# A rebuilt prologue, four units in flight and a first MLP block in halves, in a fused recurrent-attention and MLP kernel

## The chip, the cores and the metric

The kernel runs on one core of one Trainium2 chip. The metric is the time of one execution on the device, in microseconds (us), as a median over several executions. The profile takes one execution; its span is about 1.7 us shorter than the time of that same execution (226.5 against 228.2 before the change), so spans are compared with spans and times with times. "Granted clock" is the share of its full clock that TensorE was given, as the trace records it. All executions quoted here are in the fast state of the chip, but for one, which is named.

## The reference

A linear recurrence (RWKV-5) over 768 steps for 4 sequences of 8 heads with 48 channels, then an MLP with SiLU on all 3072 tokens. Cut to what matters:

```python
for t in range(S):
    kt, vt, rt = (k[:, :, t].copy(), v[:, :, t].copy(), r[:, :, t].copy())
    cur = np.einsum('bhd,bhe->bhde', u[None] * kt, vt)
    y[:, :, t] = np.einsum('bhd,bhde->bhe', rt, state + cur)
    state = w[None, :, :, None] * state + np.einsum('bhd,bhe->bhde', kt, vt)
# y, as x of 3072 x 384, goes into the MLP:
h = x @ w_in                      # 384 x 2048
g = h * (1.0 / (1.0 + np.exp(-h)))
out = g @ w_out                   # 2048 x 384
```

## The kernel before

The steps are cut into chunks of 128. A **unit** is one chunk of one sequence: 24 units, and the four units of a chunk together make one MLP **block** of 512 tokens. Each unit goes through these parts:

- "natural" products on GpSimd: ku = k·u, rku_f = r·ku, kc = k times decay powers, and, after a sum on VectorE, vu = v·rku;
- p1: r and k are transposed on TensorE (tr, tk) and scaled by decay powers on VectorE (rT, kT);
- p2: the masked attention matrix (ae, ao);
- p3: the output y and the new state st (sps is the matmul part, sdec the decayed old state, stb its half-precision copy);
- p4: y is transposed (yT) and copied by ScalarE into the MLP's input xT.

The block's matmuls (hps with w_in, ops with w_out) are "fillers": pieces that the unit loop drops between the parts of later units. In all the timelines TensorE runs everything in the order in which it is written here.

The setup, with four buffers per input, and the decay powers from logarithms and exponentials on ScalarE:

```python
    rin = [big.tile([128, H, 64], FP, name=f"rin{i}") for i in range(NIN)]
    kin = [big.tile([128, H, 64], FP, name=f"kin{i}") for i in range(NIN)]
    vin = [big.tile([128, H, D], FP, name=f"vin{i}") for i in range(NIN)]
    kc = [big.tile([128, H, 64], F16, name=f"kc{i}") for i in range(2)]
    for i in range(NIN):
        nc.vector.memset(rin[i][:, :, D:64], 0.0)
        nc.vector.memset(kin[i][:, :, D:64], 0.0)
    for i in range(2):
        nc.vector.memset(kc[i][:, :, D:64], 0.0)
    # ... cut ...
    def load(i):
        if i >= NU:
            return
        sc, b = unit(i)
        for t, src, wd in ((rin, r, 64), (kin, k, 64), (vin, v, D)):
            nc.sync.dma_start(out=t[i % NIN][:, :, 0:D],
                              in_=src[b, :, sc * C:sc * C + C, :]
                              .rearrange("h t d -> t h d"))

    load(0)
    nc.sync.dma_start(out=w_bc, in_=bass.AP(tensor=w.tensor, offset=0,
                                            ap=[[0, 128], [1, HD]]))
    nc.sync.dma_start(out=u_bc, in_=bass.AP(tensor=u.tensor, offset=0,
                                            ap=[[0, 128], [D, H], [1, D]]))
    for i in range(1, NIN):
        load(i)
    # ... cut ...
    lamR = cst.tile([PR, NP, C], FP)
    nc.scalar.activation(out=lamR, in_=eR, func=AF.Exp)
    lamK = cst.tile([PR, NP, C], FP)
    nc.scalar.activation(out=lamK, in_=eK, func=AF.Exp, scale=-1.0)
    lamC = cst.tile([128, H, D], FP)
    nc.scalar.activation(out=lamC.rearrange("p h d -> p (h d)"), in_=lnw_bc,
                         func=AF.Exp, scale=it_rev)
    wCT = cst.tile([PR, NP], FP)
    nc.scalar.activation(out=wCT, in_=lnwT, func=AF.Exp, scale=float(C))
```

The natural products and the start of the transposes:

```python
    def p1_natural(i):

        n = i % NIN
        L = live.setdefault(i, {})
        L["v16"] = wrk.tile([128, H, D], F16, name="v16", bufs=3)
        nc.scalar.copy(out=L["v16"], in_=vin[n])
        ku = wrk.tile([128, H, D], FP, name="ku")
        nc.gpsimd.tensor_tensor(out=ku, in0=kin[n][:, :, 0:D], in1=u_bc, op=ALU.mult)
        rku_f = wrk.tile([128, H, D], FP, name="rku_f")
        nc.gpsimd.tensor_tensor(out=rku_f, in0=rin[n][:, :, 0:D], in1=ku, op=ALU.mult)
        nc.gpsimd.tensor_tensor(out=kc[i % 2][:, :, 0:D], in0=kin[n][:, :, 0:D],
                                in1=lamC, op=ALU.mult)
        rku = wrk.tile([128, H], FP, name="rku")
        nc.vector.tensor_reduce(out=rku, in_=rku_f, axis=mybir.AxisListType.X, op=ALU.add)
        L["vu"] = wrk.tile([128, H, D], FP, name="vu")
        nc.gpsimd.tensor_tensor(out=L["vu"], in0=vin[n],
                                in1=rku.unsqueeze(2).broadcast_to([128, H, D]),
                                op=ALU.mult)

    def p1(i):
        n = i % NIN
        L = live.setdefault(i, {})
        tr = ps.tile([128, NP, C], FP, tag="tA", bufs=3)
        tk = ps.tile([128, NP, C], FP, tag="tA", bufs=3)
        for t, src in ((tr, rin), (tk, kin)):
            flat = src[n].rearrange("p h d -> p (h d)")
    # ... cut ...
        L["rT"] = wrk.tile([PR, NP, C], FP, name="rT")
        nc.vector.tensor_tensor(out=L["rT"], in0=tr[0:PR], in1=lamR, op=ALU.mult)
        L["kT"] = wrk.tile([PR, NP, C], FP, name="kT")
        nc.vector.tensor_tensor(out=L["kT"], in0=tk[0:PR], in1=lamK, op=ALU.mult)
        if i >= B:
            L["rT16"] = wrk.tile([PR, NP, C], F16, name="rT16")
            nc.scalar.copy(out=L["rT16"], in_=L["rT"])
```

The state, the copy into the MLP's input, and the first MLP layer:

```python
        L["y16"] = wrk.tile([128, H, D], F16, name="y16")
        nc.vector.tensor_tensor(out=L["y16"], in0=y, in1=L["vu"], op=ALU.add)
        if sc < NCH - 1:
            if sc:
                sdec = wrk.tile([PR, NP, PW], FP, name="sdec")
                nc.gpsimd.tensor_tensor(out=sdec, in0=st[b],
                                        in1=wCT.unsqueeze(2).broadcast_to([PR, NP, PW]),
                                        op=ALU.mult)
            for p0, c0 in ((0, 0), (64, D)):
                dst = st[b][p0:p0 + D, :, c0:c0 + D]
                if sc:
                    nc.vector.tensor_tensor(out=dst, in0=sps[p0:p0 + D, :, c0:c0 + D],
                                            in1=sdec[p0:p0 + D, :, c0:c0 + D], op=ALU.add)
                else:
                    nc.vector.tensor_copy(out=dst, in_=sps[p0:p0 + D, :, c0:c0 + D])
            nc.gpsimd.tensor_copy(out=st16[b], in_=st[b])
    # ... cut ...
        yT = ps.tile([128, NQ, C], F16, tag="y", bufs=2)
        yf = L["y16"].rearrange("p h d -> p (h d)")
        for q in range(NQ):
            nc.tensor.transpose(yT[:, q, :], yf[:, 128 * q:128 * q + 128], ident16)
        nc.scalar.copy(out=xts[sc][:, :, b, :], in_=yT)
    # ... cut ...
    def l1(sc, ft):
        if ft == 0:
            gts[sc] = wrk.tile([128, NFT, B * C], F16, name="gT", bufs=2)
        hps = ps.tile([128, B * C], FP, tag="moe", bufs=3)
        for q in range(NQ):
            nc.tensor.matmul(hps, win[q][:, ft * 128:(ft + 1) * 128],
                             xts[sc][:, q, :, :].rearrange("p b t -> p (b t)"),
                             start=(q == 0), stop=(q == NQ - 1))
        nc.scalar.activation(out=gts[sc][:, ft, :], in_=hps, func=AF.Silu)
```

The order of everything. The w_in weights go out (three DMAs with a cast, issued by GpSimd) right after the first unit's products, the w_out weights (four DMAs) in the second unit; a block's pieces become available only when all its four units are done:

```python
    def moe(sc):
        for ft in range(NFT):
            yield lambda ft=ft: l1(sc, ft)
        for b in range(B):
            for part in range(4):
                yield lambda b=b, part=part: l2(sc, b, part)

    fillers = []

    def fill(n):
        for _ in range(n):
            if fillers:
                fillers.pop(0)()


    p1_natural(0)
    for q in range(NQ):
        nc.gpsimd.dma_start(out=win[q], in_=moe_w_in[128 * q:128 * q + 128, :])
    p1(0)
    for i in range(NU):
        p2(i)
        fill(2)
        if i == 1:
            for g in range(4):
                nc.gpsimd.dma_start(
                    out=wout[:, 4 * g:4 * g + 4, :],
                    in_=moe_w_out[512 * g:512 * g + 512, :]
                    .rearrange("(f p) n -> p f n", p=128))
        if i + 1 < NU:
            p1_natural(i + 1)
            p1(i + 1)
        load(i + NIN)
        fill(1)
        p3(i)
        fill(2)
        p4(i)
        fill(3)
        sc, b = unit(i)
        if b == B - 1:
            fill(len(fillers))
            fillers.extend(moe(sc))
    fill(len(fillers))
```

## Time and profile before

| | before |
|---|---|
| time, median of 3 (lowest to highest) | 228.23 us (226.78 to 228.32) |
| span of the profiled execution | 226.5 us |
| first MLP matmul (hps) starts | 42.84 us |
| from there to the end | 183.7 us |
| mean granted TensorE clock | 0.955 of full speed |

The prediction below shows the page's slices and the main lines of the timelines. One view is added: the list of TensorE's waits in the kernel before. The columns are the matmul group that waited, what released it, and then the total in us, how many waits, and the longest.

```profile
PE yT L237 <- DVE y L211: 9.4, 4, 4.5
PE ae L179 <- DVE kT L169: 6.1, 1, 6.1
PE tr L165 <- DMA rin<-in_r_dram: 5.1, 1, 5.1
```

All of these waits lie before 42.84 us. A summary by stretch says the same of the rest. Its columns are the stretch, its length, then the busy time (and the number of instructions) of TensorE, its weight loads, VectorE, ScalarE and GpSimd, then the granted clock, the DMA share and GB/s:

```profile
0.00:42.84 42.84, 22.29 (x180) 18.49 (x180) 22.38 (x52) 10.57 (x19) 27.81 (x43) 0.79 1.01 184
42.84:226.50 183.66, 179.97 (x1494) 114.57 (x1492) 93.46 (x173) 83.59 (x155) 91.15 (x108) 0.99 0.35 81
```

In the second stretch TensorE is busy for 179.97 of 183.66 us, and the 3.7 us that it is not are the tail after the last matmul. A change that leaves TensorE's work as it is, like this one, can save time only in the first stretch, where TensorE idles for 20.6 us.

### The profile page before, as it was taken

Reading aid. Unit: us, or ns where it says so; the run is one execution under the profiler, and the core shown is the slowest. Engines: PE = TensorE matmul, PEld = TensorE weight load, DVE = VectorE, ACT = ScalarE, POOL = GpSimd, SP = SyncE. Lnnn points to the kernel's source line nnn. Section 1 sums busy time; section 2 is a strip of 40 time slices with the busy share of each in tenths; the row PEclk is TensorE's granted clock in tenths of the full one; section 3 lists DMA queues with packets and bytes.
Section 4 is the critical chain, followed back from the end, with each engine's and each line's share of the span. In section 5 each row is a group of like instructions: output and inputs, shape, how many; then the busy total and the mean of one; then the engine's idle time right before and its main releaser. Section 6 shows DMA issues by size and latency. Waiting matters only on the chain.

```text
span 226.5 us, 4378 instructions
## 1 busy us (share of the span) xinstructions
PE 202.3 (89%) x1672; PEld 133.1 (59%) x1672; DVE 115.8 (51%) x225; ACT 94.2 (42%) x173; POOL 119.0 (53%) x150
## 2 busy tenths in 40 slices
PE   1266298799999999999999999999999999999993
PEld 1164177456667656766665776666676557654561
DVE  6157365647368536656833865563685256420020
ACT  2521011586621378411578211866213783029500
POOL 2387975765674665667467466656746561000000
PEclk9999555799999999999999999999999999999999
DMA  5999999992216385026735053923161000110011
GB/s 95 201 196 208 204 185 176 224 186 50 58 38 139 105 177 104 3 76 137 166 77 107 0 142 98 213 48 61 38 142 69 3 0 3 69 53 16 3 69 69
DMA packets 81604, 22.69 MB, mean 100 GB/s; under 512 B 75824, under 2 KB 81200, under 8 KB 81584
## 3 DMA queue, kind: packets, MB, share of 16 engines
q1 hardware_dynamic: 79040, 19.28, 39.3%
q0 software_dynamic: 2544, 3.15, 8.0%
q8 instruction: 13, 0.21, 0.4%
q14 instruction: 7, 0.06, 0.1%
HBM read 20.84 MB, written 4.72 MB: 113 GB/s over the span
## 4 chain that ended last, share of the span: by engine, by line
PE 81%; POOL 8%; DVE 3%; issue 3%; DMA 2%; SPq 1%; DVEq 0%; POOLq 0%
PE hps L248 28%; PE ops L260 28%; PE ae L179 10%; PE tr L165 4%; PE tk L165 4%; PE yT L237 2%; DMA u_bc<-in_u_dram 2%; POOL ku L145 2%; PE y L201 2%; POOL rku_f L147 2%; PE sps L208 2%; PE y L198 2%; POOL wout L292 1%; SPq L102 1%; POOL kc L148 1%
## 5 line engine op out<-in xcount | busy, mean ns | idle before, releaser
L248 PE MATMUL hps<-xT,win 128*128 128x512 f16 x288 | 70.2, 384 | 0.0
L251 ACT ACTIVATE gT<-hps 128x512 f16<-128x512 f32 x96 | 57.4, 598 | 29.5 <-PE hps L248 27.3
L260 PE MATMUL ops<-wout,gT 128*128 128x384 f16 x384 | 69.0, 326 | 0.0
L260 PEld LDWEIGHTS <-gT 128*128 128x128 f16 x384 | 35.8, 98 | 21.2
L248 PEld LDWEIGHTS <-win 128*128 128x128 f16 x288 | 26.7, 99 | 26.5 <-issue 1.3
L186 DVE TENSOR_TENSOR am<-ae,maskM 128x512 f16<-128x512 f32 x24 | 16.6, 691 | 49.1 <-PE ao L181 49.1
L153 POOL TENSOR_TENSOR vu<-vin,rku 128x384 f32<-128x384 f32 x24 | 19.9, 829 | 35.8 <-DVE rku L151 35.8
L179 PE MATMUL ae<-rT,kT 48*128 48x128 f32 x192 | 30.8, 306 | 6.1 <-DVE kT L169 6.1
L179 PEld LDWEIGHTS ae<-rT,kT 48*128 48x128 f32 x192 | 25.8, 206 | 14.2 <-issue 7.5
L264 DVE COPY osb<-ops 128x384 f32<-128x384 f32 x24 | 13.4, 557 | 38.3 <-PE ops L260 37.9
L181 PE MATMUL ao<-rT,kT 48*128 48x128 f32 x192 | 30.8, 306 | 0.0
L238 ACT COPY xT<-yT 128x384 f16<-128x384 f16 x24 | 11.4, 476 | 43.3 <-PE yT L237 43.3
L145 POOL TENSOR_TENSOR ku<-kin,u_bc 128x384 f32<-128x384 f32 x24 | 24.1, 1005 | 7.9 <-DMA u_bc<-in_u_dram 6.7
L172 ACT CAST rT<-rT 112x512 f16<-112x512 f32 x20 | 12.4, 618 | 37.2 <-DVE rT L167 37.2
L181 PEld LDWEIGHTS ao<-rT,kT 48*128 48x128 f32 x192 | 25.8, 206 | 0.0
L147 POOL TENSOR_TENSOR rku_f<-rin,ku 128x384 f32<-128x384 f32 x24 | 24.0, 999 | 1.9
L148 POOL TENSOR_TENSOR kc<-kin,lamC 128x384 f16<-128x384 f32 x24 | 24.0, 999 | 0.8 <-ACT lamC L130 0.8
L225 POOL CAST stb<-st 112x384 f16<-112x384 f32 x20 | 10.1, 503 | 25.0 <-DVE st L221 19.9
L165 PE MATMUL tr<-ident,rin 128*112 128x128 f32 x96 | 16.7, 302 | 5.1 <-DMA rin<-in_r_dram 5.1
L167 DVE TENSOR_TENSOR rT<-tr,lamR 112x512 f32<-112x512 f32 x24 | 16.5, 689 | 4.2 <-PE tr L165 4.2
L151 DVE TENSOR_REDUCE rku<-rku_f 128x8 f32<-128x384 f32 x24 | 13.1, 544 | 10.2 <-POOL rku_f L147 10.1
L165 PEld LDWEIGHTS tr<-ident,rin 128*112 128x112 f32 x96 | 12.5, 147 | 9.0 <-issue 5.9
(46 smaller groups left out, 200.9 us busy)
## 6 DMA issues: line engine op xcount, KB each, us to landing
rin<-in_r_dram SPq DMA_DIRECT2D x24, 192.0 KB, 3.4
kin<-in_k_dram SPq DMA_DIRECT2D x24, 192.0 KB, 3.5
vin<-in_v_dram SPq DMA_DIRECT2D x24, 192.0 KB, 3.6
out_dram<-osb SPq DMA_DIRECT2D x24, 192.0 KB, 1.9
win<-in_moe_w_in_dram POOLq DMA_DIRECT2D x3, 512.0 KB, 8.8
wout<-in_moe_w_out_dram POOLq DMA_DIRECT2D x4, 384.0 KB, 10.3
w_bc<-in_w_dram SPq DMA_DIRECT2D x1, 192.0 KB, 4.3
u_bc<-in_u_dram SPq DMA_DIRECT2D x1, 192.0 KB, 4.1
```

The costliest lines, as they stand in the source:

```text
L145: nc.gpsimd.tensor_tensor(out=ku, in0=kin[n][:, :, 0:D], in1=u_bc, op=ALU.mult)
L147: nc.gpsimd.tensor_tensor(out=rku_f, in0=rin[n][:, :, 0:D], in1=ku, op=ALU.mult)
L148: nc.gpsimd.tensor_tensor(out=kc[i % 2][:, :, 0:D], in0=kin[n][:, :, 0:D], in1=lamC, op=ALU.mult)
L153: nc.gpsimd.tensor_tensor(out=L["vu"], in0=vin[n], in1=rku.unsqueeze(2).broadcast_to([128, H, D]), op=ALU.mult)
L165: nc.tensor.transpose(t[0:PR, p, :], flat[:, 128 * p:128 * p + PR], ident)
L167: nc.vector.tensor_tensor(out=L["rT"], in0=tr[0:PR], in1=lamR, op=ALU.mult)
L179: nc.tensor.matmul(ae[:, p, :], L["kT"][0:D, p, :], L["rT"][0:D, p, :], start=True, stop=True)
L181: nc.tensor.matmul(ao[:, p, :], L["kT"][64:PR, p, :], L["rT"][64:PR, p, :], start=True, stop=True)
L186: nc.vector.tensor_tensor(out=am, in0=a, in1=maskM.unsqueeze(1).broadcast_to([128, NP, C]), op=ALU.mult)
L248: nc.tensor.matmul(hps, win[q][:, ft * 128:(ft + 1) * 128], xts[sc][:, q, :, :].rearrange("p b t -> p (b t)"), start=(q == 0), stop=(q == ...
L251: nc.scalar.activation(out=gts[sc][:, ft, :], in_=hps, func=AF.Silu)
L260: nc.tensor.matmul(ops, gts[sc][:, ft, b * C:(b + 1) * C], wout[:, ft, :], start=(ft == 0), stop=(ft == NFT - 1))
```

## The change

The intent was to shorten that first stretch:

- the inputs of the first four units go out first, the weights after them: w_in in 12 pieces, w_out two units later, and the load of the fifth unit is held back, by an added dependency, until GpSimd's last product of the fourth unit ("the weights go first");
- the decay powers come from repeated doubling on VectorE and no longer from exponentials on ScalarE;
- four units are in flight, each at another part (p1 of unit s, p2 of s-1, p3 of s-2, p4 of s-3);
- the first MLP block is split into two halves of two units, so that the MLP could start after two units and not after four;
- PSUM is one ring of eight buffers in place of three pools (3, 2 and 3).

The diff, cut to its core:

```diff
+    NKC = 3
+    def load(i, after=None):
 ...
+            if after is not None:
+                tc.add_manual_dep(d.ins, after.ins.name, ...,
+                                  reason="the weights go first")
 ...
+    for i in range(NIN):
+        load(i)                                  # r, k, v of four units, first on SyncE's queue
 ...
-    lamR = cst.tile([PR, NP, C], FP)
-    nc.scalar.activation(out=lamR, in_=eR, func=AF.Exp)
-    lamK = cst.tile([PR, NP, C], FP)
-    nc.scalar.activation(out=lamK, in_=eK, func=AF.Exp, scale=-1.0)
+    n = 1
+    while n < C:
+        for t, o in ((pw, 1), (iw, 0)):
+            nc.vector.tensor_tensor(
+                out=t[:, :, o + n:o + 2 * n], in0=t[:, :, o:o + n],
+                in1=t[:, :, o + n - 1:o + n].broadcast_to([PR, NP, n]), op=ALU.mult)
+        n *= 2
 ...
-        tr = ps.tile([128, NP, C], FP, tag="tA", bufs=3)
+        tr = ps.tile([128, NP, C], FP, name="tr", tag="ps", bufs=8)      # and so for all PSUM tiles
 ...
+    blocks = ([Block([0, 1]), Block([2, 3])]
+              + [Block(list(range(B * sc, B * sc + B))) for sc in range(1, NCH)])
 ...
-    p1_natural(0)
-    for q in range(NQ):
-        nc.gpsimd.dma_start(out=win[q], in_=moe_w_in[128 * q:128 * q + 128, :])
-    p1(0)
-    for i in range(NU):
-        p2(i)
-        fill(2)
-        if i == 1:
+    for s in range(NU + 3):
+        if s < NU:
+            p1(s)
+            natural(s)
+        if s == 1:
+            for g in range(4):
+                for q in range(NQ):
+                    nc.gpsimd.dma_start(out=win[q][:, 512 * g:512 * g + 512],
+                                        in_=moe_w_in[128 * q:128 * q + 128,
+                                                     512 * g:512 * g + 512])
+        if s == 3:
             for g in range(4):
                 nc.gpsimd.dma_start(out=wout[:, 4 * g:4 * g + 4, :], ...)
 ...
+        if s == 0:
+            for b in range(B):
+                nc.gpsimd.memset(st[b], 0.0)
         fill(2)
+        if 0 <= s - 1 < NU:
+            p2(s - 1)
+        fill(2)
+        if s < NU:
+            bonus(s)                             # rku and vu
+        if s == 3:
+            load(4, after=last_pool[3])          # last_pool[3] is vu of unit 3
+            load(5)
+            load(6)
+        elif s > 3:
+            load(s + 3)
+        if 0 <= s - 2 < NU:
+            p3(s - 2)
+        fill(2)
+        if 0 <= s - 3 < NU:
+            p4(s - 3)
+            bl = block_of[s - 3]
+            if s - 3 == bl.units[-1]:
+                fillers.extend(moe(bl))
+        fill(2)
```

A filler of the first layer weighs 1 for a whole block and 0.5 for a half block, all others weigh 1, so a stage of four fill(2) takes up to eight units of weight.

## The prediction

> **What bounds the kernel now.** I read the page's slices first, then TensorE's order of time, then those of GpSimd and of the SyncE queue.
>
> ```profile
> span 226.5 us, 4378 instructions
> PE   1266298799999999999999999999999999999993
> PEclk9999555799999999999999999999999999999999
> DMA  5999999992216385026735053923161000110011
> ```
>
> Each digit is 5.66 us. From slice 8 to the end TensorE is full; only the first 45 us have room, and there the 16 DMA engines are full and the granted clock falls to half in slices 5 to 7.
>
> ```profile
> 42.84 2.73 PE L248 MATMUL hps<-xT,win 128*128 128x512 f16 x6
> ...
> 61.47 0.60 PE L165 MATMUL tr<-ident,rin 128*112 128x128 f32 x4
> ...
> 69.52 0.60 PE L165 MATMUL tr<-ident,rin 128*112 128x128 f32 x4
> ...
> 202.05 10.36 PE hps L248 x48
> 212.41 10.41 PE ops L260 x64
> ```
>
> (The last two are from the chain that ended last, the rest from TensorE's timeline.) The first MLP matmul starts at 42.84. One unit then takes 69.52 - 61.47 = 8.05 us without a gap, and an MLP block (48 + 64 matmuls) is 20.8 us, so 5.2 us a unit; attention is the other 2.85. So the time is "start of the MLP" plus TensorE work that nobody interrupts, plus a tail of 3.7 us (last matmul 222.8, span 226.5). The change can win only before the start of the MLP, or lose by making holes after it.
>
> ```profile
> 13.69 1.81 POOL L285 DMA_DIRECT2D win<-in_moe_w_in_dram  x3
> 20.99 3.06 POOL L292 DMA_DIRECT2D wout<-in_moe_w_out_dram  x4
> 36.72 1.00 POOL L145 TENSOR_TENSOR ku<-kin,u_bc 128x384 f32<-128x384 f32 x1 [1.13 <-DMA kin<-in_k_dram]
> 15.04 8.21 SPq L102 DMA_DIRECT2D kin<-in_k_dram  x1
> 23.35 4.57 SPq L102 DMA_DIRECT2D vin<-in_v_dram  x1
> 28.02 4.85 SPq L102 DMA_DIRECT2D rin<-in_r_dram  x1
> DMA to landing us min/median/max: 3.2/3.5/21.6
> ```
>
> (GpSimd's and SyncE's timelines; the last line is of kin's transfers in the first 60 us.) GpSimd pays for each weight DMA: 0.55 us for the first kind, 0.77 for the second. The fifth k tile was issued at 15.04 and landed at 36.6, because it shared the DMA engines with the weights; the median is 3.5.
>
> **What the skill says.** "DMA: Bandwidth & Descriptors", Queues, rings and completion order: each engine takes its queue rows in turn, a packet at a time. The trace agrees: with both kinds queued, the small-packet inputs (192-byte rows) fell from one tile per about 1 us to one per 4.5 us (SyncE's issues at 23.35, 28.02, 32.97). Same page, SWDGE vs HWDGE vs iDMA: a cast in the DMA must be issued from GpSimd, in software; the trace shows the 0.55 and 0.77 us. "TensorE: Matmul & The Clock Gate", Part 1: idle TensorE runs at half rate until some 3.4 us of work. The trace agrees: the ae/ao pairs come every 0.21 us at 13 to 17 us and every 0.11 later.
>
> **The change, part by part.**
>
> Powers by doubling: 2 exponentials of 0.6 us and 2 products of 0.69 go, 16 small VectorE operations come, and they need only wpT (landed at 3.3), not the ACT table. rT(0), before at 11.7, can start near 6. This gates nothing later: GpSimd is slower.
>
> Inputs first: SyncE starts with r, about 0.9 us earlier; u goes by ACT's queue. So the first ku starts near 5.4 instead of 9.14. Four units of input (12 tiles at 0.96 us) are in by about 15.
>
> GpSimd's sum decides when the rest may come. From the compiled order up to the last product of unit 3: ku 1.07, rku 0.96, kc 0.96, vu 0.8 = 3.8 per unit, four units 15.2; a wait for lamC 0.4; four state memsets, moved from VectorE, about 0.4 each (estimate from the 0.20 of 128 columns) 1.6; the w_in weights, now 12 DMAs of 128 rows instead of 3, 12 x 0.55 = 6.6 instead of 1.8; one cast of the state 0.5; w_out 4 x 0.77 = 3.1. 5.4 + 27.4 = 32.8 us. w_out's issues lie at 28.9 to 32.0 (before 21.0 to 24.0): later by 8 us.
>
> The new dependency lets load(4), r of unit 4, go only after that last product: at 32.8, before it was at 14.3. w_out alone would take about 8.5 us of full engines (10.8 us in the old trace, less 2.3 for two input tiles in it), from 30.5 to 39, and r and k of unit 4 share with it at 4.5 us a tile as long as it lasts. r lands near 39.5, k near 42 (old: 31.7 and 36.6).
>
> TensorE runs in order, and at stage 4 its order is: transposes of unit 4, p2 of unit 3, p3 of unit 2, the transpose of unit 1, then the first half block. Cold: k's transposes 0.9, p2 1.7, p3 0.9, yT 0.45, the copy on ACT 0.5. So the MLP starts at about 42 + 4.5 = 46.5, against 42.84, although it needs only units 0 and 1.
>
> After the start: before, 226.5 - 42.8 = 183.7, of which 1.3 was half clock (6 matmuls in 2.6 us instead of 1.3). More is left over than before: one p2 (0.95), one p3 (0.57), two yT (0.34), together 1.9. The half blocks cost 48 more matmuls of half width, streaming the same columns: 0.2. The start will again be partly cold, 0.4. Sum 183.7 - 1.3 + 1.9 + 0.2 + 0.4 = 184.9.
>
> Stages of four in flight: VectorE's and GpSimd's results are now used one stage later. In the old trace TensorE already had no gap there, so nothing is won. The early halves also run out: the order has no MLP matmuls in stages 9 and 10. TensorE has 2.84 us a stage there and GpSimd 5.1; the lag of a stage hides most of it, I add 0.5.
>
> One PSUM ring of 8: 15 tiles a stage in the first-layer stages, so each waits for what was released half a stage (4 us) before; no cost expected.
>
> Sum: 46.5 + 184.9 + 0.5 = 231.9 us of span. The timed runs lie 1.7 above the span (228.2 against 226.5): 233.6. I take something off, to 232.0, as the contention with w_out may be milder than in the old trace.
>
> **The rivals.**
>
> First: the intent succeeds. Inputs without contention, halves that start after two units, and the MLP starts in the low thirties; time about 218 to 222. For it: the old trace's DMA row is full for 40 us and k of unit 4 was 21.6 us on its way. Against it: GpSimd's 27 us of work in front of load(4), and TensorE's order, which puts unit 4 in front of the first half block. It would need weight DMAs far cheaper than 0.55 us when they are 512 columns; but 512 rows cost 0.77 and 128 rows 0.55, so it is rows and a fixed part that count, not bytes.
>
> Second: load(4) still waits for GpSimd at 32.8, but w_out doesn't slow it: r at 36, k at 36.5, start at 41, span 226.5, time 228: same.
>
> Third: the holes in stages 9 and 10 show. GpSimd's 5.1 us against 2.84 over two stages is up to 4.5 us more: 236. Against it: GpSimd may work ahead as far as its buffers go, in the eight-microsecond stages before.
>
> Fourth: the last four w_in issues wait for the landing of the first four, one DMA semaphore each. If those are slow, GpSimd stands still and everything moves by 1 to 3 us: 234 to 236.
>
> **Range and chances.** The start of the MLP is uncertain by about 3 us either way (41 if the second rival holds, 48 with the fourth), the rest by 1 to 2. 80% range 227.5 to 236. The border for slower is 232.8, just above my value; for faster 223.7, which needs a start at 37. Faster 0.07, same 0.50, slower 0.43.
>
> **What would show it.** GpSimd's timeline: win x12 for about 6.6 us from near 14, wout near 29, vu of unit 3 ending near 33. SyncE: r of unit 4 waiting for POOL vu until then. TensorE: a wait of over 10 us in front of tr of unit 4, "DMA rin", ending near 39 to 42, and the first hps near 46; from there no idle time but a little near stages 9 and 10. I'm wrong if tr of unit 4 starts before 36 (cheaper issues or no contention), or if TensorE shows gaps of over 2 us in total after the MLP has begun.

## The result

| | before | after |
|---|---|---|
| time, median (lowest to highest) | 228.27 us (226.78 to 230.17), 4 runs | 248.51 us (248.09 to 249.69), 4 runs |
| span of the profiled execution | 226.5 us | 248.0 us |
| first MLP matmul starts | 42.84 us | 51.90 us |
| from there to the end | 183.7 us | 196.1 us |
| mean granted clock | 0.955 | 0.924 |

The kernel became slower: the ratio is 1.089, with a 95% interval of 1.080 to 1.098. Here and below a ratio is the mean time of the one kernel's fast runs over the mean time of the kernel before's fast runs of the same rounds, so it is not quite the ratio of the medians. The prediction had said 232.0, with a range of 227.5 to 236. The profile divides the 21.5 us of span: 9.1 us before the first MLP matmul (51.90 - 42.84) and 12.4 us after it (196.1 - 183.7).

The slices of the page after, each digit now 6.2 us:

```profile
PE   2691000599999994999999999999999999999994
PEclk9998555559999998899999999999999999999999
DMA  7999639999174379530747903479101100010011
```

TensorE is nearly empty in four slices in a row (3 to 6, counted from 0: the digits 1, 0, 0, 0), has a short hole in slice 15 (the 4, near 95 us), and shows nothing else in this coarse row. The DMA row is no longer full at the start: in slices 4 and 5 it falls to 6 and 3, just where TensorE is empty. In the six microseconds from 28.5 to 34.5 hardly anything moves on either: TensorE is busy for 0.5 us, and the DMA share is 0.03. TensorE's waits after:

```profile
PE tr L172 <- DMA rin<-in_r_dram: 20.2, 2, 16.0
PE yT L254 <- DVE y L219: 10.0, 1, 10.0
PE hps L263 <- ACT xT L255: 7.0, 7, 3.6
```

The first line has the one long wait that the prediction named, 16.0 us for r of the fifth unit. The third is new: hps waits seven times for xT; six of these come after the MLP has begun. GpSimd's timeline shows why r came so late (start, duration, the work; in brackets the idle time before it and what ended it):

```profile
10.17 1.00 POOL L151 TENSOR_TENSOR kc<-kin,lamC 128x384 f16<-128x384 f32 x1 [1.98 <-ACT lamC L134]
...
16.32 5.51 POOL L310 DMA_DIRECT2D win<-in_moe_w_in_dram  x10
22.86 0.53 POOL L310 DMA_DIRECT2D win<-in_moe_w_in_dram  x1 [1.02 <-DMA win<-in_moe_w_in_dram]
24.93 0.53 POOL L310 DMA_DIRECT2D win<-in_moe_w_in_dram  x1 [1.54 <-DMA win<-in_moe_w_in_dram]
...
33.51 3.05 POOL L315 DMA_DIRECT2D wout<-in_moe_w_out_dram  x4
36.54 0.87 POOL L160 TENSOR_TENSOR vu<-vin,rku 128x384 f32<-128x384 f32 x1
```

GpSimd waits 1.98 us for a decay table (lamC), then takes from 16.32 to 25.46, 9.1 us, for the twelve w_in issues, with two waits for the landing of earlier pieces inside. In the compiled program the ninth issue takes the semaphore of the first again, the tenth that of the second, and so on in a cycle of eight; so an issue must wait until the transfer eight before it has landed. Three plus four weight DMAs, as before, never meet this. The vu at 36.54 is the product that the added dependency names. SyncE's queue obeys it:

```profile
37.44 0.37 SPq L68 DMA_DIRECT2D rin<-in_r_dram  x1
```

r of unit 4 goes out at 37.44 and lands at 45.9, 8.3 us later by the trace's transfer times. TensorE takes up work there, and its first half block follows six microseconds later:

```profile
45.91 1.07 PE L172 MATMUL tr<-ident,rin 128*112 128x128 f32 x4 [15.96 <-DMA rin<-in_r_dram]
...
51.90 4.00 PE L263 MATMUL hps<-xT,win 128*128 128x256 f16 x18 [0.57 <-ACT xT L255]
```

The eighteen half-width matmuls take 4.00 us here, and the same group takes 2.13 us once TensorE is warm (at 70.81 us): the clock was at half, as the PEclk row shows up to slice 8.

Now the second part of the loss. The stretches of the kernel after that answer to those of before:

```profile
0.00:51.90 51.90, 18.42 (x146) 14.48 (x147) 21.22 (x55) 7.67 (x13) 31.84 (x55) 0.72 1.04 142
51.90:248.00 196.10, 185.94 (x1574) 123.15 (x1573) 96.08 (x180) 87.21 (x173) 93.84 (x111) 0.98 0.42 78
```

After the MLP has begun TensorE is now busy 6.0 us longer (185.94 against 179.97) and idle 6.5 us longer (196.10 - 185.94 = 10.2 against 3.7). The idle time is one wait of 3.64 us and five of 0.57 us, 6.5 us in all, each in front of the first hps of a block or half block. The large one, in order of time over all engines:

```profile
92.77 0.33 PE L254 MATMUL yT<-ident,y 128*128 128x128 f16 x3
92.93 0.83 POOL L223 TENSOR_TENSOR sdec<-st,pw 112x384 f32<-112x384 f32 x1
93.80 0.73 DVE L229 TENSOR_TENSOR st<-sps,sdec 48x192 f32<-48x192 f32 x2 [1.27 <-POOL sdec L223]
94.56 0.69 DVE L174 TENSOR_TENSOR rT<-tr,pw 112x512 f32<-112x512 f32 x1
...
95.28 0.62 ACT L179 CAST rT<-rT 112x512 f16<-112x512 f32 x1 [4.02 <-DVE rT L174]
...
96.22 0.47 ACT L255 COPY xT<-yT 128x384 f16<-128x384 f16 x1
```

TensorE has its last transpose done at 93.1. The copy to xT needs 0.47 us, but ScalarE takes its work in the order of the program, and two casts stand ahead of the copy; the first of them waits for VectorE's rT, which stands behind VectorE's st, which waits for GpSimd's sdec. So the block waits for GpSimd, through three in-order queues. GpSimd is busy nearly all the time in these stages: its vu starts at 86.13, 92.15 and 98.12, so a stage takes 6.0 us there, while TensorE has only 2.84 us of attention work in it and no MLP piece to fill the rest. Two lines of GpSimd's timeline show its own waits in these stages:

```profile
86.13 0.83 POOL L160 TENSOR_TENSOR vu<-vin,rku 128x384 f32<-128x384 f32 x1 [2.04 <-DVE rku L157]
...
94.66 0.50 POOL L233 CAST stb<-st 112x384 f16<-112x384 f32 x1 [0.89 <-DVE st L229]
```

The second wait comes in each of these stages: the 5.1 us of GpSimd's work and these 0.89 us for VectorE's st are the 6.0 us. The first shows why GpSimd had not worked ahead: in the last stages that still had fillers it waited 2.78 and 2.04 us for VectorE's sum rku.

In the kernel before, the same stretch had no hole; the columns are those of the summary by stretch:

```profile
80.00:100.00 20.00, 20.00 (x172) 12.70 (x172) 10.37 (x21) 11.23 (x22) 12.94 (x16) 1.00 0.40 84
```

The kernel after:

```profile
80.00:100.00 20.00, 16.36 (x166) 11.81 (x164) 13.61 (x27) 5.74 (x12) 15.10 (x18) 0.94 0.74 124
```

The account of the 12.4 us, each figure from the timelines. At the start of the MLP, 2.2 us for half clock (18 hps in 3.8 us from start to start of what follows, and 1.96 us at full clock, plus four transposes in 0.84 and not 0.44). The hole at 93 to 97 us costs 3.8 us from start to start, 1.7 us because the matmuls behind it run at half clock again (nine hps in 3.1 us in place of 1.94, the transposes after them in 0.85), and 0.3 us in the stage before: 5.8 us. Five gaps of 0.73 us from start to start, of which 0.57 is shown as a wait for xT, stand at the other block starts: 3.65 us. That is 11.65 us; the remaining 0.8 us is what the prediction's own sum had (1.9 us of attention work left over, 0.2 us for halves, less 1.3 us for half clock that the kernel before had there itself).

### The profile page after: what moved, and what is told of

It reads as the page before. It is cut to its first block, busy times and chain, and to the rows that moved or that the text cites. A ratio compares the mean times of both kernels' runs of the same rounds, so it can differ in the third digit from the quotient of the medians.

```text
span 248.0 us, 4555 instructions
## 1 busy us (share of the span) xinstructions
PE 204.4 (82%) x1720; PEld 137.6 (56%) x1720; DVE 117.3 (47%) x233; ACT 94.9 (38%) x185; POOL 125.7 (51%) x166
## 4 chain that ended last, share of the span: by engine, by line
PE 72%; POOL 12%; DMA 9%; issue 3%; ACT 2%; DVE 1%; SPq 0%; POOLq 0%; DVEq 0%
PE hps L263 27%; PE ops L275 24%; PE ae L186 8%; DMA kin<-in_k_dram 4%; PE tr L172 4%; DMA rin<-in_r_dram 3%; PE tk L172 3%; POOL rku_f L150 2%; POOL ku L148 2%; POOL kc L151 2%; DMA win<-in_moe_w_in_dram 2%; POOL vu L160 2%; PE y L208 2%; PE yT L254 1%; PE sps L216 1%
## 5 line engine op out<-in xcount | busy, mean ns | idle before, releaser
L263 PE MATMUL hps<-xT,win 128*128 128x512 f16 (+1 forms) x336 | 72.0, 361 | 7.0 <-ACT xT L255 7.0
L266 ACT ACTIVATE gT<-hps 128x512 f16<-128x512 f32 (+1 forms) x112 | 57.8, 536 | 22.3 <-PE hps L263 20.6
L263 PEld LDWEIGHTS <-win 128*128 128x128 f16 x336 | 32.5, 101 | 32.3 <-issue 7.3
L172 PE MATMUL tr<-ident,rin 128*112 128x128 f32 x96 | 17.2, 310 | 22.6 <-DMA rin<-in_r_dram 20.2
L174 DVE TENSOR_TENSOR rT<-tr,pw 112x512 f32<-112x512 f32 x24 | 16.6, 690 | 34.9 <-PE tr L172 34.8
L179 ACT CAST rT<-rT 112x512 f16<-112x512 f32 x20 | 12.4, 618 | 46.8 <-DVE rT L174 46.8
L186 PE MATMUL ae<-rT,kT 48*128 48x128 f32 x192 | 29.9, 300 | 0.0
L188 PE MATMUL ao<-rT,kT 48*128 48x128 f32 x192 | 29.8, 299 | 0.0
L186 PEld LDWEIGHTS ae<-rT,kT 48*128 48x128 f32 x192 | 25.1, 200 | 7.9 <-DVE kT L176 3.5
L188 PEld LDWEIGHTS ao<-rT,kT 48*128 48x128 f32 x192 | 25.0, 200 | 0.0
L229 DVE TENSOR_TENSOR st<-sps,sdec 48x192 f32<-48x192 f32 x32 | 11.4, 355 | 18.9 <-POOL sdec L223 13.0
```

Of the source, the lines that this page charges most:

```text
L172: nc.tensor.transpose(t[0:PR, p, :], flat[:, 128 * p:128 * p + PR], ident)
L186: nc.tensor.matmul(ae[:, p, :], L["kT"][0:D, p, :], L["rT"][0:D, p, :], start=True, stop=True)
L188: nc.tensor.matmul(ao[:, p, :], L["kT"][64:PR, p, :], L["rT"][64:PR, p, :], start=True, stop=True)
L263: nc.tensor.matmul(hps[:, 0:n], win[q][:, ft * 128:(ft + 1) * 128], bl.xT[:, q, 0:bl.n, :].rearrange("p b t -> p (b t)"), start=(q == 0), ...
L266: nc.scalar.activation(out=bl.gT[:, ft, 0:n], in_=hps[:, 0:n], func=AF.Silu)
```

## The experiments

The theory to be tested: (1) the start is late because GpSimd's work stands in front of the load of unit 4, through the dependency; w_in in twelve pieces and w_out's transfer beside r make it worse; (2) the hole near 95 us comes from fillers that run out; (3) the gaps of 0.73 us come from the transposes of a block's last unit standing directly in front of its first hps. The rivals: the halves as such are at fault; the PSUM ring or the doubling costs something; the lost time is fixed and only moves when one cause is taken away. Not run alone are the four units in flight; the version with three repairs and whole blocks, which has them, comes out at the time of the kernel before. Where a recorded expectation speaks of theories A and B, the letters hold for that experiment alone. All kernels of the experiments gave correct results. "Rest" is the span less the start of the first hps.

Two cautions for the table. Span, start and rest come from one execution each: that of the kernel after was the slowest of its four (249.69 us), that of the run without the dependency the fastest of its four (234.05 us). The ratios use all fast runs. And the rest is not the same work everywhere: with the transposes first, 1.5 us of attention work (p2 of unit 3, p3 of unit 2) come after the first hps instead of before it; with a whole first block less attention work is left when the MLP starts.

| experiment | time, median | ratio to before (95%) | span | first hps | rest |
|---|---|---|---|---|---|
| before (profile) | 228.27 | 1 | 226.5 | 42.84 | 183.7 |
| after | 248.51 | 1.089 (1.080 to 1.098) | 248.0 | 51.90 | 196.1 |
| no dependency | 235.30 | 1.025 (1.020 to 1.031) | 232.3 | 36.41 | 195.9 |
| w_in in 3 | 240.85 | 1.051 (1.046 to 1.056) | 239.7 | 44.87 | 194.8 |
| w_out later | 242.21 | 1.059 (1.053 to 1.064) | 240.7 | 43.60 | 197.1 |
| transposes first | 243.92 | 1.065 (1.059 to 1.071) | 242.9 | 47.39 | 195.5 |
| whole blocks | 245.12 | 1.069 (1.063 to 1.074) | 243.4 | 59.28 | 184.1 |
| even filling alone | 242.47 | 1.060 (1.055 to 1.065) | 241.2 | 50.82 | 190.4 |
| before, new prologue alone | 228.95 | 1.000 (0.996 to 1.005) | 227.1 | 42.66 | 184.4 |
| before, one ring alone | 228.87 | 0.999 (0.994 to 1.005) | 227.3 | 43.37 | 183.9 |
| three repairs | 227.35 | 0.995 (0.989 to 1.000) | 225.0 | 30.95 | 194.1 |
| three repairs, whole blocks | 229.01 | 1.002 (0.997 to 1.007) | 226.6 | 43.65 | 183.0 |
| three repairs, even filling (second run) | 220.52 | 0.964 (0.959 to 0.968) | 218.7 | 30.82 | 187.9 |

### The load of unit 4 without its dependency

```diff
-            load(4, after=last_pool[3])
+            load(4)
```

> The changed kernel without the dependency that lets r of unit 4 go only after the last product of unit 3. Theory A (that dependency makes the late start): r and k of unit 4 are issued from about 13.4 us, when unit 0's buffers are free, and land before the w_in weights are under way, near 17 to 20; TensorE's stage 4 then waits for GpSimd only (rku_f of unit 3 ends at 32.6, so y of unit 1 is ready near 34), the first hps comes near 35 instead of 51.9; span 248 - 16 = about 232 (229 to 238). Theory B (contention between small input packets and weights is what matters, the dependency only moves it): k of unit 4 lands as late as in the kernel before (36.6) or later because w_in is in its way, the first hps comes at 44 or later, and the span stays above 240.

Measured: 235.30 us, span 232.3, as theory A has it. TensorE's timeline has the first half block here:

```profile
36.41 3.76 PE L263 MATMUL hps<-xT,win 128*128 128x256 f16 x18 [2.03 <-ACT xT L255]
```

The start is 15.5 us earlier than in the kernel after, and the span 15.7 us shorter, so nothing of it is given back later. These are the slowest execution of the one and the fastest of the other; by the ratios (1.089 to 1.025) it is 14.5 us, by the medians 13.2. The dependency is the largest single cost, about two thirds of the whole loss. Without it the MLP even starts 6.4 us before the kernel before's, so the early halves do what they are meant to; the rest of 195.9 us is as bad as it was, and that is why the result is still slower.

### w_in in three DMAs

```diff
-            for g in range(4):
-                for q in range(NQ):
-                    nc.gpsimd.dma_start(out=win[q][:, 512 * g:512 * g + 512],
-                                        in_=moe_w_in[128 * q:128 * q + 128,
-                                                     512 * g:512 * g + 512])
+            for q in range(NQ):
+                nc.gpsimd.dma_start(out=win[q], in_=moe_w_in[128 * q:128 * q + 128, :])
```

> The changed kernel with the w_in weights in 3 DMAs instead of 12, all else kept. Theory A (GpSimd's sum of work in front of the dependency): 9.1 us of issuing and waiting (16.32 to 25.46) become 1.7, so the last product of unit 3 ends near 30 instead of 37.4 and r of unit 4 is issued there; the first hps comes 6 to 7 us earlier, near 45 to 46; span about 241 (239 to 244). Theory B (the weights' transfer sets it): w_in and w_out must be through anyway, r and k of unit 4 then share the engines longer, the first hps moves by less than 3 us; span above 245.

Measured: 240.85 us, span 239.7, first hps at 44.87, as theory A has it. GpSimd's timeline of this kernel:

```profile
16.52 1.82 POOL L309 DMA_DIRECT2D win<-in_moe_w_in_dram  x3
...
26.40 3.05 POOL L312 DMA_DIRECT2D wout<-in_moe_w_out_dram  x4
```

The three issues take 1.82 us in place of 9.1, and everything behind them moves up by 7.1 us (w_out from 33.51 to 26.40). A DMA issue cost 0.55 to 0.6 us of GpSimd whether it carried 512 or 2048 columns, so cutting w_in into pieces cost four times the issue time and two waits besides. The first hps moves by 7.0 us, one for one with GpSimd: the dependency makes GpSimd's sum the start of the MLP.

### w_out's issues one stage later, the dependency kept

```diff
-        if s == 3:
+        if s == 4:
             for g in range(4):
                 nc.gpsimd.dma_start(out=wout[...], ...)
```

> The changed kernel, dependency and all kept, with the four w_out DMAs issued one stage later, behind the three products of unit 4, so that nothing of the weights is on the DMA engines when r and k of unit 4 are let go. It measures the disputed contention. Theory A (sharing with w_out costs r and k of unit 4 the 4 to 5 us that their landing is over the median): load(4) goes at 37.4 - 3.1 = 34.3; r lands 3 to 4 us later, near 37.7, k near 39, and the first hps comes near 43 to 44 instead of 51.9; w_out lands near 50 to 52, before or just when the second layer wants it; span 240 to 242. Theory B (no contention, the late issue is all): r still takes 8 us, the first hps moves by the 3.1 us of w_out's issue only, to 48.5; span near 245.

Measured: 242.21 us, span 240.7, first hps at 43.60. In this kernel GpSimd's w_out issues stand behind the dependency, so r of unit 4 has the DMA engines nearly to itself. SyncE's issue, and TensorE's answer to it:

```profile
34.17 0.37 SPq L68 DMA_DIRECT2D rin<-in_r_dram  x1
...
37.59 1.07 PE L172 MATMUL tr<-ident,rin 128*112 128x128 f32 x4 [7.87 <-DMA rin<-in_r_dram]
```

As expected. r took 3.3 us from issue to landing; in the kernel after it took 8.3. So of the 8.3 us by which the first hps came earlier, 3.3 are the issue time of w_out taken from in front of the load, and 5.0 are the contention of w_out's transfer with r's small rows. It costs little elsewhere: TensorE waits 0.8 us for w_out later.

### The transposes at the head of the stage

```diff
     for s in range(NU + 3):
+        if 0 <= s - 3 < NU:
+            p4(s - 3)
+            bl = block_of[s - 3]
+            if s - 3 == bl.units[-1]:
+                fillers.extend(moe(bl))
 ...
-        if 0 <= s - 3 < NU:
-            p4(s - 3)
-            ...                                  # the same five lines, from before the last fill
```

> The changed kernel with the transpose of unit s-3 (and its copy) put at the head of the stage, before the transposes of unit s. Theory A (what is lost after the start of the MLP comes from the copy xT being needed at once, and in the hole from ACT's order, xT of unit 7 behind rT of unit 10): the five gaps of 0.73 us go except the last (3), the gap of 3.8 us in front of block 1 goes or falls under 1, with the cold matmuls behind it (1.7); and the first hps comes right after the transposes of unit 4, near 48 instead of 51.9 (3.5). Together 8 to 11 us: span 237 to 240. Theory B (the hole is GpSimd's pace of 5.1 us a stage against TensorE's 2.84, order does not matter): only the gaps of 0.73 and the earlier start, 5 to 6 us: span 242 to 243, and the gap before block 1 stays over 2 us.

Measured: 243.92 us, span 242.9. This hit the rival's figure; the favoured 237 to 240 was missed. TensorE's waits in this kernel, the longest wait in the stretch that answers to the hole, and that stretch:

```profile
PE yT L254 <- DVE y L219: 14.1, 3, 11.3
...
PE yT L254 <- DMA rin<-in_r_dram: 2.0, 1, 2.0
PE hps L263 <- ACT xT L255: 0.6, 1, 0.6
```

```profile
84.53 0.50 PE L254 MATMUL yT<-ident,y 128*128 128x128 f16 x3 [1.98 <-DMA rin<-in_r_dram]
```

```profile
79.54:93.05 13.51, 10.39 (x98) 9.20 (x97) 9.63 (x20) 3.50 (x7) 10.25 (x13) 0.67 0.94 176
```

The waits for xT fall from 7.0 to 0.6 us, so the cause of the gaps is as stated: transposes, copy and first hps stood in a row. But the hole in the stages without fillers did not go: there TensorE waits for y and for r in place of xT, is idle for 3.1 of 13.51 us, and runs at a clock of 0.67: the clock is at half for some 10 us, from 84.1 to 94.4, though no wait there is longer than 1.98 us. The rest falls by 0.6 us only (196.1 to 195.5); the other 4.5 us come from an earlier first hps. As 1.5 us of work moved from the start to the rest, the gain on equal work is some 3.0 us at the start and 2.1 us in the rest. Where the transposes stand does not decide about the hole; that fits GpSimd as the pace of those stages, and the two runs with even filling test it.

### The first block whole

```diff
-    blocks = ([Block([0, 1]), Block([2, 3])]
-              + [Block(list(range(B * sc, B * sc + B))) for sc in range(1, NCH)])
+    blocks = [Block(list(range(B * sc, B * sc + B))) for sc in range(NCH)]
```

> The changed kernel with the first MLP block whole (units 0 to 3) instead of in halves. Theory A (halves help the start but leave stages 9 and 10 without MLP work): the hole before block 1 goes (3.8 + 1.7 + 0.3 us), one gap of 0.73 fewer, but the first hps has to wait for stages 5 and 6, near 61 instead of 51.9, in which only 3 to 4 us of TensorE work are done more; span 248 - 6.5 + 9 - 4 = 246 to 248. If halves are the fault on balance it is below 243; if they are a clear gain it is above 251.

Measured: 245.12 us, span 243.4, first hps at 59.28; this falls between two of the expectation's answers (246 to 248 for theory A, below 243 for halves as the fault), so neither was hit. The MLP starts 7.4 us later, but the rest is 184.1 us, nearly that of the kernel before (183.7). So in the kernel after the halves lose on balance 4.6 us: they take fillers early and leave none for stages 9 and 10. This by itself does not say whether halves are bad or only their use; the last two experiments do.

### The kernel before with the new prologue, and with the new ring

The first of the two takes the setup of the kernel after (u and w by ScalarE's queue, loads of four units first, powers by doubling, the pad memsets) with the old loop and NKC = 2. The second changes the PSUM pools alone:

```diff
-        tr = ps.tile([128, NP, C], FP, tag="tA", bufs=3)
+        tr = ps.tile([128, NP, C], FP, name="tr", tag="ps", bufs=8)
 ...                                             # and so for tk, ae, ao, y, sps, yT, hps, ops
```

> The kernel before with only the setup of the changed one: powers by doubling, u and w by ACT's queue, inputs of four units issued first, pad memsets moved; stages, weights' places, blocks and PSUM pools as before. Theory (the setup gains 2 to 3 us at the first rT and ku, but the inputs of unit 4 come when the weights let them, as before): the first hps moves by 0 to 3 us, 40 to 43; time within 1.5% of before, ratio 0.985 to 1.005. Rival (the setup itself is a loss, as w and u land later behind four tiles of input: wpT landed at 5.3 instead of 3.3): first hps later, ratio 1.01 or more.

> The kernel before with the single ring of 8 PSUM buffers in place of the pools of 3, 2 and 3; nothing else. Theory (TensorE had no gap from PSUM before, and one ring of 8 is reused after about 4 us): same within 1%, ratio 0.99 to 1.01. Rival (the ring makes TensorE wait for buffers held by VectorE in order): slower by over 1%, with waits of tr, ae or hps for VectorE or ACT that the kernel before does not have.

Measured: 228.95 us (ratio 1.000) and 228.87 us (ratio 0.999). With the new prologue rT of unit 0 starts at 9.94 in place of 11.71 us, and the first hps at 42.66 in place of 42.84: the 1.8 us won by doubling do not reach the MLP. The ring adds no wait for a buffer to TensorE's list. Neither part is worth or costs anything by itself within the intervals of half a per cent, as the prediction had said of the doubling and of the ring.

### Three repairs together

The dependency removed, w_in in three DMAs, the transposes at the head: the three edits above in one kernel.

> The changed kernel with three repairs at once: no dependency for load(4), w_in in 3 DMAs, transposes of unit s-3 at the head of the stage; halves kept. Theory (the losses are separate and add): w_in's 7.5 us of GpSimd time go from in front of unit 2, so that the inputs of unit 4 and not GpSimd set the start; first hps near 32 (before 36.4 without the dependency alone); then 184.5 us of TensorE work, the hole in stages 9 and 10 still about 5, cold matmuls 2: span about 224 (220 to 228), about the time of the kernel before. Rival: w_in whole in the rings at 17 us starves the inputs of unit 4 for as long as it lasts, and the first hps stays at 36 or later: span 228 or more.

Measured: 227.35 us, ratio 0.995, span 225.0, first hps at 30.95: as expected. The start is now 11.9 us before the kernel before's, and 10.4 us of it are lost in the rest (194.1 against 183.7). By stretch, TensorE is busy for 186.24 of the 194.05 us: of the 10.4 us, 4.1 are idle time (7.8 less the tail of 3.7) and 6.3 are work left over or slower work (186.24 less 179.97).

### Fewer fillers per stage up to stage 9

On top of the three repairs:

```diff
     for s in range(NU + 3):
+        FR = 1.25 if s < 10 else 2
 ...
-        fill(2)
+        fill(FR)                                # all four
```

> The same three repairs, and in stages 0 to 9 only 5 instead of 8 MLP pieces a stage, so that the two half blocks last until block 1 is ready. Theory (the hole is GpSimd's and VectorE's pace of 6.0 us a stage against 2.84 us of TensorE work without filling; the amount of work is the same, so spreading it fills the hole): 2.84 + 5 x 0.65 = 6.1 us a stage, no gap over 1 us after the first hps, and no half clock there; span 4 to 7 us below the run with the three repairs, about 218. Rival (the waits come from order and buffers, not from too little filling): no change, within 2 us.

> The kernel with three repairs and even filling once more, unchanged, for its profile (the profiled execution of the first time was a stray one of 1127 us) and a narrower interval. Theory: first hps near 31 as with the three repairs, no idle time over 1 us after it, span near 217.7; time near 219.4, ratio 0.955 to 0.963. If gaps of more than 2 us in total remain after the first hps, the account of start + 184.5 + cold is wrong.

Measured at first: 219.12, 219.31 and 219.40 us in three fast runs, ratio 0.959. The fourth, which was the profiled one and was marked slow, took 1127.5 us with TensorE some five times slower throughout; it is left out of every figure, and it was the only one of its kind in the study. For a usable profile the same kernel was run again with more rounds: 220.52 us (219.01 to 221.46, six runs), ratio 0.964, where 0.955 to 0.963 was expected. In that second profile all of TensorE's waits lie before 30.82 us, the first hps. From there to the end:

```profile
30.82:218.70 187.88, 184.17 (x1603) 122.04 (x1601) 98.30 (x184) 87.14 (x175) 96.80 (x114) 0.99 0.48 92
```

TensorE is idle only for the tail of 3.7 us. Spreading the same fillers over more stages took 4.1 us of idle time and 2.1 us of slow matmuls (186.24 to 184.17 us busy) out of the three-repairs kernel. This version is 3.6% faster than the kernel before and 11% faster than the kernel after.

### The even filling alone

The same edit on the kernel after, with nothing else changed.

> The changed kernel with 5 instead of 8 MLP pieces a stage in stages 0 to 9, all else as it is. It isolates the hole. Theory A (two stages without MLP work run at 6.0 us a stage and let the clock fall): the gap of 3.8 us before block 1 and the 2.0 us of half clock behind it go, the start stays at 51.9: span 248 - 5.8 = 242 (241 to 243.5). Theory B (ACT's order in that stage, xT of unit 7 behind the casts of unit 10, makes the gap): the wait for xT before block 1 stays over 2 us and the span above 245.

Measured: 242.47 us, span 241.2, as theory A has it. The waits for xT in this kernel:

```profile
PE hps L263 <- ACT xT L255: 3.4, 6, 0.6
```

The wait of 3.6 us is gone, and what is left are the six of 0.57 us. The rest falls from 196.1 to 190.4 us, by 5.7 us; the account above had put 5.8 us on the hole with its half clock. Fillers that ran out are the cause, shown in isolation, and the waits of 0.57 us are another matter. The span fell by 1.1 us more than that, because the first hps came at 50.82 and not at 51.90. The edit does not touch that part: here only the twelfth w_in issue waited, 1.76 us, where two had waited 2.56 us in the profile of the kernel after. So a start can differ by about 1 us from one execution to the next.

### Three repairs with whole blocks

The three repairs, and the first block whole.

> The three repairs with the first block whole instead of halves. Theory (GpSimd's 5 to 6 us a stage decides when unit 3 is through): the first hps comes with unit 3, near 41 to 43, but more attention work is done by then (179 instead of 184.5 us left), no hole: span 221 to 225, as the halves with the hole. If halves were the better form in themselves, this would be over 4 us behind the run with the three repairs.

Measured: 229.01 us, ratio 1.002, first hps at 43.65. This missed the expectation: the start came 0.65 us after the latest that was expected (41 to 43), and the span of 226.6 us lies 1.6 us above the expected 221 to 225. With the three repairs, then, halves win 12.7 us at the start (43.65 to 30.95), lose 11.1 us afterwards with the old filling, and only 4.9 us with the even one (187.9 against 183.0); a part of both losses is attention work that is still to be done when the MLP starts earlier. The halves are worth having, provided their fillers are spread.

## Why the prediction was wrong, point by point

The path up to the start of the MLP was right, and its size was not; for what follows the start, the mechanism was wrong too: GpSimd was taken to need 5.1 us a stage and to work ahead, and TensorE to have no idle time but 0.5 us. 232.0 us was predicted and 248.5 came, with both terms of the sum too small, the start by 5.4 us (51.9 for 46.5) and what follows by 10.7 us (196.1 for 185.4). The prediction had given "same" 0.50 and "slower" 0.43. Of its own two signs of being wrong, one came: TensorE had 6.5 us of gaps after the start of the MLP, where over 2 us was the sign.

- **"12 x 0.55 = 6.6"** is the first step that failed. The issues took 9.1 us: the price of one was right (6.6 us for the twelve without their waits), but two of them waited 1.02 and 1.54 us for landings. The prediction had this as its fourth rival, with "1 to 3 us" and a time of "234 to 236", and left it out of its value. The three-DMA run confirms the weight of the whole term: 7.0 us of start.
- **"A wait for lamC 0.4"** measured 1.98 us, and the first ku started at 6.03, not at 5.4. The memsets, "1.6", took 1.5. Together with w_in this makes the load of unit 4 go 4.6 us later than "32.8" (vu of unit 3 ends at 37.4).
- **The dependency** was seen and its mechanism held: r waits for GpSimd's vu, TensorE waits 16.0 us for r, and then 4.9 us of in-order work (predicted 4.5) precede the half block. The run without it moves the start by 15.5 us. k of unit 4 landed 9.6 us after r's issue, where 9.2 was predicted ("42" less "32.8").
- **"I take something off, to 232.0, as the contention with w_out may be milder"** was wrong, and so was the second rival, that w_out doesn't slow it. r took 8.3 us beside w_out and 3.3 us without it.
- **"I add 0.5"** for stages 9 and 10 measured 5.8 us; this was the most costly step. The third rival ("up to 4.5 us more: 236") had the right kind of sum, but a stage of GpSimd took 6.0 us and not the 5.1 of its work: it waits 0.89 us for VectorE's st, and the timeline of the kernel before, which the prediction had read, shows that wait already (1.2 us before stb). The argument against the rival, that GpSimd may work ahead as far as its buffers go, did not hold: in the stages before, GpSimd waited 2.78 and 2.04 us for VectorE's rku. And after the hole of 3.8 us the clock was at half for the next 3 us, which no term had. The even filling alone shows it: 5.7 us less in the rest.
- **"No idle time but a little near stages 9 and 10"** missed the five gaps of 0.73 us. In the new order the transposes of a block's last unit and its first hps stand next to each other, with a copy on ScalarE between; in the old order fill(3) and p2 of the next unit lie between them. No term of the sum looked at what stands next to what. The run with the transposes first takes the waits for xT away but for one of 0.6 us, yet its rest gains only 0.6 us, or 2.1 on equal work, for the 3.65 us of gaps and the hole together.
- **"The start will again be partly cold, 0.4"** measured 2.2 us: the clock had been at half since 22.4 us, through waits of 10.0 and 16.0 us, and the first 18 hps ran at it.
- **"No cost expected"** of the ring and **"this gates nothing later"** of the doubling both held, at ratios of 0.999 and 1.000.
- The first rival (the MLP starts "in the low thirties; time about 218 to 222") is what the repaired kernel does: 30.8 us and 220.5 us. The prediction was right that the change as written could not get there, and right that GpSimd's work in front of the load would be why.

On the Trainium skill: "TensorE: Matmul & The Clock Gate", section "HAM oscillation — how this bites in real kernels", warns of idle stretches of over some 3.4 us, after which matmuls run at half rate; the hole of 3.8 us and the nine hps behind it (3.1 us in place of 1.94) agree with it, and the gaps of 0.73 us were not followed by slow matmuls. Two other runs do not agree: with the transposes first, and with the three repairs, the clock fell to half in or just after a wait of 1.98 us, the longest in its stretch, and stayed there for some 10 and 3.4 us. So the 3.4 us are no safe limit here.

What stays open: that the gaps turn, in the kernel with the transposes first, into waits for y and r at half clock was read from its waits and not tested further; why there the clock stayed at half for 10 us; whether the transposes first are needed at all once the filling is even, since no run left only them out; and the cause of the one run of 1127.5 us.

## What to carry to other kernels

Before a load is made to wait for something, add up what the engine that releases it has to do until then; here one added dependency turned 31 us on GpSimd (6.0 to 37.4) into the start of the whole MLP and cost some 14.5 us (13.2 by the medians, 15.7 by the spans). Work that fills another engine's waits is a stock: starting it earlier gains only if it is also spent more slowly, up to the stage in which the next stock comes. And when an order is rewritten, look for every chain of transposition, copy and use that has become adjacent, and for every in-order queue in which a short copy now stands behind a long wait.

## What the Trainium skill lacked or had wrong

- "DMA: Bandwidth & Descriptors", section "Anatomy of one DMA — SWDGE (gpsimd) path", calls descriptor generation "small, variable" and puts the fixed cost on completion. For a kernel whose GpSimd is busy the issue itself counts: 0.55 us of GpSimd for a DMA of 128 rows at 512 columns (5.51 for ten), 0.61 us (1.82 for three) at 2048 columns, 0.76 us (3.05 for four) for 512 rows of 384 columns. In these three it goes by DMAs and rows, hardly by bytes.
- No page looked at says that a long train of DMAs can make its issuing engine wait for its own earlier transfers. In the compiled program the semaphores of GpSimd's DMAs come round after eight, and the eleventh and twelfth issue waited 1.02 and 1.54 us.
- "DMA: Bandwidth & Descriptors", section "Queues, rings and completion order", tells of turns by packets but gives no figure for a transfer of small rows beside large ones: 192 KB in rows of 192 bytes took 8.3 us to landing beside w_out, and 3.3 us without it.
- "TensorE: Matmul & The Clock Gate", section "HAM oscillation — how this bites in real kernels", puts the idle stretch to be avoided at over some 3.4 us: with the transposes first a wait of 1.98 us, the longest in its stretch, went with half clock for some 10 us.
- No page looked at tells of a whole execution several times slower than its neighbours: one of 1127.5 us among runs of 219 us. Its trace holds no record of the clock at all (the 1.0 in its result stands for that), so that it ran at full clock is not shown.
